# Reordering the last loads and the middle weight load of a two-layer decode attention kernel, with the program order of the last head pair to match

## The chip, the cores and the metric

The kernel runs on one core of one Trainium2 chip. The metric is the device time of one execution in microseconds (us). A profile is one further execution, and its clock starts at the span's start. Its page is the summary that the profiler prints of it. Engines: PE is the tensor engine, PEld its weight load, DVE the vector engine, ACT the scalar engine, SP the engine that issues the loads.

The runs were spread over several chips. Ratios are always taken against the kernel before, on the same chip and in the same rounds. The profiles shown are single executions.

## The reference

Two independent decode attention layers, A and B, of the same shape, each for one token (cut; A and B differ only in their data):

```python
# x [1,1,512], k_cache and v_cache [1,32,8192,128], wq [512,4096], wo [4096,512], all bf16
q = (x @ wq).reshape(B, Sq, H, Dh).transpose(0, 2, 1, 3)
scores = einsum("bhqd,bhkd->bhqk", q, k_cache) * Dh ** -0.5
p = softmax(scores, axis=-1)
o = einsum("bhqk,bhkd->bhqd", p, v_cache)
out = o.transpose(0, 2, 1, 3).reshape(B, Sq, H * Dh) @ wo
# result: concatenate([out_A, out_B], axis=-1)
```

K and V of both layers are 64 heads of 2 MB each; with the weights 285 MB are read once. There is hardly any arithmetic per byte.

## The kernel before

The heads are taken in 32 pairs (16 of A, then 16 of B). K of pair j is called Kj, V of pair j is Vj; each is a 4 MB load. All loads go through one ring of five 4 MB slots in a fixed order, and a load is issued as soon as the load five places earlier has been used up:

```python
order = [('wq', a) for a in range(NA)]
for j in range(NPR + 1):                   # NPR = 32 pairs, PPA = 16 pairs a layer
    if j < NPR:
        order.append(('k', j))
    if 1 <= j <= NPR:
        if j == NPR:
            order.append(('wo', NA - 1))   # woB, between V30 and V31
        order.append(('v', j - 1))
    if j == PPA:
        order.append(('wo', 0))            # woA, behind V15
LAST_PARTS = [(0, 64), (64, 96), (96, 112), (112, 128)]   # V31 comes in four loads
...
if n >= NS:                                # NS = 5 slots
    for ctr, val in free_of[n - NS]:
        W('SP', ctr, val)
```

For a pair, DVE multiplies K by q in eight pieces (`plan_M`), PE sums over parts of the head dimension with an identity matrix (`plan_fold`, two halves of 16 matmuls), DVE reduces (`plan_R`), and a softmax follows over DVE, PE and ACT (`plan_m1` to `plan_ri`). `plan_PV` multiplies V by p: 128 matmuls of two columns, each with its own 128x128 weight load. `plan_o` scales. `plan_w` permutes the result of a block of heads on PE and DVE, and `plan_y` multiplies it with rows of wo.

Every engine runs its own list in the order in which the plan functions were called. The order of before (cut):

```python
for j in range(NPR + 1):
    ...                                    # M(j), fold(j,0) .. softmax of j-1 .. fold(j,1), R(j,0)
    if j == NPR:                           # behind the last pair's softmax:
        for h0, n, pm in wo_plan[NA - 1]:  # w and y of B's heads 0..27 (16 + 8 + 4)
            if pm and (NA - 1) * PPA + (h0 + n) // 2 - 1 <= j - 2:
                plan_w(NA - 1, h0, n)
                plan_y(NA - 1, h0, n, pm)
    if c:
        plan_PV(j - 1)
    if j == PPA + 1:                       # j = 17: w and y of A behind PV of pair 16
        for h0, n, pm in wo_plan[0]:
            plan_w(0, h0, n)
            plan_y(0, h0, n, pm)
plan_o(NPR - 1)
for h0, n, pm in wo_plan[NA - 1]:          # y of B's last four heads
    if not pm:
        plan_y(NA - 1, h0, n, pm)
```

## Time and profile before

Median 691.01 us (690.29 to 692.37, three runs). The span of the profile is 688.0 us.

| what | number | read from |
|---|---|---|
| HBM bytes | 285.2 MB, 415 GB/s over the span | the page, part 3 |
| rate where the stream is full | 423 to 437 GB/s in nearly all slices | the page, row GB/s |
| DVE idle for K loads | most of 179.4 us, 6 us a pair | the page, groups |
| nothing issued by SP | 360.1 to 395.0 us | timeline of SP |
| last landing, y_sb, end | 675.8, 683.2, 688.0 us | completions, timeline |

The page's row of GB/s in 40 slices of 17.2 us, and two of its groups (line, engine, operation, tiles, count, then busy us and mean ns, then idle time before them and its releaser):

```profile
GB/s 366 440 433 436 423 426 430 430 437 430 431 428 430 428 430 430 432 429 435 432 428 426 371 425 396 420 430 428 431 428 433 424 433 433 430 432 431 421 408 47
L360 DVE TENSOR_TENSOR ring<-ring,qbc 128x2048 bf16<-128x2048 bf16 x256 | 300.7, 1215 | 179.4 <-DMA ring<-in_B_k_cache_dram 93.1
L458 PE MATMUL otps<-p,ring 128*128 128x2 bf16 x4096 | 108.2, 163 | 0.6 <-issue 0.6
```

The stream is flat but for the first slice, a dip in the middle (371, 396) and the last slices. The Trainium skill, "DMA: Bandwidth & Descriptors", section Specifications, gives a fabric ceiling of 435 GB/s; the trace agrees, with about 430 in most slices.

The dip, in the timeline of SP's issues (start, duration, what), and in windows of 5 us (window, length, busy of PE, PEld, DVE, ACT, POOL with counts, granted PE clock with 1.00 for full speed, DMA share, GB/s):

```profile
356.92 0.33 SPq L262 DMA_DIRECT2D ring<-in_B_k_cache_dram  x1
360.11 0.33 SPq L262 DMA_DIRECT2D ring<-in_B_v_cache_dram  x1
394.97 0.33 SPq L262 DMA_DIRECT2D ring<-in_B_k_cache_dram  x1
```

```profile
385.00:390.00 5.00, 2.93 (x110) 2.72 (x106) 2.36 (x4) 0.00 (x0) 0.00 (x0) 0.90 1.02 436
390.00:395.00 5.00, 4.40 (x128) 4.35 (x128) 0.41 (x2) 0.00 (x0) 0.00 (x0) 0.50 0.61 259
395.00:400.00 5.00, 0.26 (x1) 0.13 (x2) 5.00 (x7) 0.00 (x0) 0.00 (x0) 0.50 0.86 321
```

SP has nothing to issue for 35 us, because K19 needs the slot of woA and woA is used up only by y of A, which PE ends at 395. The queue runs dry on the way.

The tail, in the chain of work that ended last (start, duration, what):

```profile
609.17 35.89 DMA ring<-in_B_k_cache_dram
...
658.83 5.21 PE fold L373 x16
664.03 3.21 PE otps L458 x128
...
667.42 0.61 DVE s_sb L386
...
671.21 0.58 PE stps L435 x2
671.80 0.43 PE qwps L496 x16
672.23 1.02 issue
673.25 2.26 PE yps L536 x64
...
678.80 3.43 PE otps L458 x128
...
682.47 0.71 PE yps L536 x16
683.21 0.16 DVE y_sb L545
```

K31 lands at 645.06. The last fold ends at 664, then come PV of pair 30, the softmax of pair 31 (to 671.8), w and y of 28 heads (to 678.8) and all of PV of pair 31, though V31 had landed at 675.8.

### The profile page before, as it was taken

What the parts mean: (1) busy time and instruction counts of PE and PEld (TensorE: products, weight loads), DVE (VectorE), ACT (ScalarE), POOL (GpSimd) and SP (SyncE); (2) the same over time, 40 slices, a digit from 0 to 9 for tenths busy, and PEclk for the clock granted to TensorE, in tenths of its full rate; (3) what the DMA queues carried; (4) which work ended last, traced back from release to release, by engine and by line L of the source; (5) the groups of instructions that cost most, each with busy time, mean ns of one, the idle gap of its engine ahead of it and who ended that gap; (6) DMA issues with size and microseconds to landing.
All of it is one profiled execution on the core that took longest, in us unless ns stands there. A gap on an engine that the chain in (4) does not pass through costs nothing.

```text
span 688.0 us, 12357 instructions
## 1 busy us (share of the span) xinstructions
PE 467.0 (68%) x5660; PEld 260.8 (38%) x5660; DVE 377.6 (55%) x513; ACT 42.5 (6%) x169; POOL 2.4 (0%) x16
## 2 busy tenths in 40 slices
PE   0487687767776766766683767756776676777675
PEld 0134443433444433433341634423443442443345
DVE  4158655664655566646535385566565456664621
ACT  0110000000000000000000000000000000000010
POOL 1000000000000000000000000000000000000000
PEclk9999877987778776888776878777788776788775
DMA  9999999999999999999999899999999999999991
GB/s 366 440 433 436 423 426 430 430 437 430 431 428 430 428 430 430 432 429 435 432 428 426 371 425 396 420 430 428 431 428 433 424 433 433 430 432 431 421 408 47
DMA packets 11667, 286.00 MB, mean 416 GB/s; under 512 B 1760, under 2 KB 2272, under 8 KB 2656
## 3 DMA queue, kind: packets, MB, share of 16 engines
q1 hardware_dynamic: 11328, 285.22, 97.1%
q8 instruction: 44, 0.72, 0.4%
q10 hardware_dynamic: 288, 0.00, 0.0%
q14 instruction: 7, 0.06, 0.0%
HBM read 285.21 MB, written 0.00 MB: 415 GB/s over the span
## 4 chain that ended last, share of the span: by engine, by line
DMA 57%; PE 28%; DVE 11%; issue 2%; ACT 1%; ACTq 0%; DVEq 0%
DMA ring<-in_B_k_cache_dram 27%; DMA ring<-in_A_k_cache_dram 26%; PE fold L373 17%; DVE ring L360 10%; PE otps L458 6%; DMA xT<-in_B_x_dram 3%; PE qwps L332 2%; PE yps L536 1%; ACT qbc L339 1%; DVE m L409 1%; ACT p L428 0%; DVE wt L503 0%; DVE w_bf L512 0%; PE stps L404 0%; PE qwps L496 0%
## 5 line engine op out<-in xcount | busy, mean ns | idle before, releaser
L360 DVE TENSOR_TENSOR ring<-ring,qbc 128x2048 bf16<-128x2048 bf16 x256 | 300.7, 1215 | 179.4 <-DMA ring<-in_B_k_cache_dram 93.1
L373 PE MATMUL fold<-ring,ident 128*128 128x512 bf16 x1024 | 308.3, 469 | 126.5 <-DVE ring L360 126.4
L373 PEld LDWEIGHTS fold<-ring,ident 128*128 128x128 bf16 x1024 | 114.0, 117 | 295.6 <-DVE ring L360 131.9
L458 PEld LDWEIGHTS otps<-p,ring 128*128 128x128 bf16 x4096 | 108.3, 96 | 8.0 <-issue 0.7
L458 PE MATMUL otps<-p,ring 128*128 128x2 bf16 x4096 | 108.2, 163 | 0.6 <-issue 0.6
L386 DVE TENSOR_REDUCE s_sb<-fold 128x64 f32<-128x512 f32 x64 | 42.9, 671 | 7.5 <-PE fold L373 7.2
L409 DVE TENSOR_REDUCE m<-stps 2x1 f32<-2x128 f32 x32 | 8.9, 279 | 67.4 <-PE stps L404 67.4
L420 ACT COPY nb<-stps 128x1 f32<-128x1 f32 x32 | 5.1, 159 | 586.2 <-PE stps L414 586.2
L435 PE MATMUL stps<-rowsum,ones_f 128*128 128x2 f32 x64 | 12.6, 267 | 41.5 <-ACT p L428 41.5
L332 PE MATMUL qwps<-ring,xsel 128*128 128x512 bf16 x64 | 16.5, 405 | 29.3 <-DVE xsel L225 24.4
L428 ACT ACTIVATE p<-s_sb,nb 64x128 bf16<-64x128 f32 x64 | 27.9, 436 | 2.1 <-ACT nb L420 0.3
L435 PEld LDWEIGHTS stps<-rowsum,ones_f 128*128 128x128 f32 x64 | 9.9, 194 | 44.2 <-ACT p L428 44.2
L332 PEld LDWEIGHTS qwps<-ring,xsel 128*128 128x128 bf16 x64 | 6.0, 103 | 39.3 <-issue 27.3
L414 PE MATMUL stps<-m,sel 2*128 2x1 f32 x64 | 12.3, 259 | 11.9 <-DVE m L409 11.9
L414 PEld LDWEIGHTS stps<-m,sel 2*128 2x128 f32 x64 | 9.6, 186 | 24.5 <-DVE m L409 24.5
L396 DVE TENSOR_REDUCE m<-s_sb 64x1 f32<-64x128 f32 x64 | 17.7, 277 | 1.0
L474 DVE TENSOR_TENSOR ot<-otps,rinv 128x2 bf16<-128x2 f32 x32 | 4.9, 152 | 15.6 <-PE otps L458 15.6
L428 ACT ACTIVATION_READ_ACCUMULATOR p<-s_sb,nb 64x1 f32 x64 | 11.7, 182 | 0.0
L536 PE MATMUL yps<-w_bf,ring 128*128 128x1 bf16 x240 | 8.6, 172 | 3.8 <-DVE w_bf L512 2.8
L536 PEld LDWEIGHTS yps<-w_bf,ring 128*128 128x128 bf16 x240 | 8.3, 118 | 4.1 <-issue 2.9
L404 PE MATMUL stps<-ident_f,m 128*2 128x128 f32 x32 | 8.7, 273 | 1.5 <-DVE m L396 1.5
L225 DVE TENSOR_SCALAR xsel<-parity,xT 128x256 bf16<-128x256 bf16 x8 | 1.7, 282 | 12.2 <-DMA xT<-in_B_x_dram 12.2
(30 smaller groups left out, 34.9 us busy)
## 6 DMA issues: line engine op xcount, KB each, us to landing
ring<-in_A_k_cache_dram SPq DMA_DIRECT2D x16, 4096.0 KB, 37.2
ring<-in_A_v_cache_dram SPq DMA_DIRECT2D x16, 4096.0 KB, 31.9
ring<-in_B_k_cache_dram SPq DMA_DIRECT2D x16, 4096.0 KB, 37.7
ring<-in_B_v_cache_dram SPq DMA_DIRECT2D x15, 4096.0 KB, 32.4
ring<-in_A_wq_dram SPq DMA_DIRECT2D x1, 4096.0 KB, 12.5
ring<-in_B_wq_dram SPq DMA_DIRECT2D x1, 4096.0 KB, 22.0
ring<-in_A_wo_dram SPq DMA_DIRECT2D x1, 4096.0 KB, 38.8
ring<-in_B_wo_dram SPq DMA_DIRECT2D x1, 2048.0 KB, 33.3
```

Of the source, the lines that this page charges most:

```text
L332: m = e.matmul(qw_ps[:, :].rearrange("p (j d) -> p j d", d=Dh), xsel[:, a, c, par, :], wq[:, c, 4 * g:4 * g + 4, par, :], start=(i == 0), ...
L360: m_val[(j, i)] = INC('DVE', c_m, lambda e: e.tensor_tensor(t, t, qbc[:, a, jj:jj + 1, :].broadcast_to([P, CH, Dh]), ALU.mult))
L373: m = e.matmul(fold_ps[h][:, :].rearrange("p (t e) -> p t e", e=FE), ident[:], t[:, h * HT:(h + 1) * HT, c * FE:(c + 1) * FE], start=(c == ...
L386: r_val[(j, h)] = INC('DVE', c_r, lambda e: e.tensor_reduce(s_sb[:, j % 2, h * HT:(h + 1) * HT], fold_ps[h][:, :].rearrange("p (t e) -> p ...
L396: m1_val[j] = INC('DVE', c_m1, lambda e, h=h, q0=q0, q1=q1: e.tensor_reduce(m1[q0:q1, j % 2, h:h + 1], s_sb[q0:q1, j % 2, :], AX.X, ALU.max))
L404: tr_val[j] = INC('PE', c_tr, lambda e: e.transpose(st_ps[j % 2][0:2, 0:P], m1[:, j % 2, :], ident_f[:]))
L409: m2_val[j] = INC('DVE', c_m2, lambda e: e.tensor_reduce(m2[0:2, j % 2:j % 2 + 1], st_ps[j % 2][0:2, 0:P], AX.X, ALU.max))
L414: bc_val[j] = INC('PE', c_bc, lambda e: e.matmul(st_ps[j % 2][:, P:P + 1], sel2[:], m2[0:2, j % 2:j % 2 + 1], start=True, stop=True))
L428: e_val[j] = INC('ACT', c_e, lambda e, h=h, q0=q0, q1=q1: e.activation(p2[q0:q1, j % 2, :, h], s_sb[q0:q1, j % 2, :], AF.Exp, bias=nb[q0:q ...
L435: s_val[j] = INC('PE', c_s, lambda e: e.matmul(st_ps[j % 2][:, P + 2:P + 4], ones_f[:], rowsum[:, j % 2, :], start=True, stop=True))
L458: m = e.matmul(ot_ps[j % 2][:, 0:2], t[:, i, :], p2[:, j % 2, i, :], start=(i == 0), stop=(i == TP - 1))
L536: m = e.matmul(y_ps[:, b:b + 1], wo[:, h0 + i, :, b], src[:, a, h0 + i:h0 + i + 1], start=(first and i == 0 and b == 0), stop=(lastblk and ...
```

## The change

Its intent has two parts. In the middle, woA is loaded two pairs later (behind V17) and y of A is done one pair later, so that no load waits for y of A while the queue runs dry. At the end, the loads come in the order K31, woB, V30, V31, and everything that needs neither V30 nor V31 (the softmax of pair 31, y of 28 heads) is planned ahead of PV of pair 30. The core of the diff:

```diff
-            if 1 <= j <= NPR:
-                if j == NPR:
-                    order.append(('wo', NA - 1))
+            if j == NPR - 1:
+                order.append(('wo', NA - 1))
+            if j >= 1:
                 order.append(('v', j - 1))
-            if j == PPA:
+            if j == PPA + 2:
                 order.append(('wo', 0))
 ...
+                if j == PPA + 1:
+                    for h0, n, pm in wo_plan[0]:
+                        plan_w(0, h0, n)
+                if j == PPA + 2:
+                    for h0, n, pm in wo_plan[0]:
+                        plan_y(0, h0, n, pm)
 ...
+        j = NPR - 1
+        plan_R(j, 1)
+        plan_w_ready(j - 2)
+        ys = list(perm_l)
+        plan_y(LA, *ys.pop(0))
+        plan_m1(j)
+        plan_tr(j)
+        if ys:
+            plan_y(LA, *ys.pop(0))
+        plan_m2(j)
+        plan_bc(j)
+        plan_exp(j)
+        plan_sum(j)
+        plan_ri(j)
+        for b in ys:
+            plan_y(LA, *b)
+        for i in range(2):
+            plan_PV(j - 1 + i)
+            plan_o(j - 1 + i)
+            plan_y(LA, *direct_l[i])
```

(B's last four heads become two blocks of two; w of B's heads is done in the loop as soon as its o is there.)

More of the change, by code (lines that the diff above doesn't have):

```diff
@@ L92, in bass_concat_heads__mha_block_cached__gqa_block_cached__decode_kernel @@
             h0 += n
-        if h0 < H:
-            blocks.append((h0, H - h0, False))
+        while h0 < H:
+            blocks.append((h0, 2, False))
+            h0 += 2
         wo_plan.append(blocks)
@@ L560, in bass_concat_heads__mha_block_cached__gqa_block_cached__decode_kernel, with plan_w_ready @@
                 plan_q(a, g)
-        for j in range(NPR + 1):
-            k = j < NPR
+        LA = NA - 1
+        perm_l = [b for b in wo_plan[LA] if b[2]]
+        direct_l = [b for b in wo_plan[LA] if not b[2]]
+        w_done = set()
+        def plan_w_ready(jo):
+            for h0, n, pm in perm_l:
+                if h0 not in w_done and LA * PPA + (h0 + n) // 2 - 1 <= jo:
+                    w_done.add(h0)
+                    plan_w(LA, h0, n)
+        for j in range(NPR):
             c = 0 <= j - 1
-            if k:
-                for i in range(4):
-                    plan_M(j, i)
+            for i in range(4):
+                plan_M(j, i)
             if j >= 2:
@@ L570, in bass_concat_heads__mha_block_cached__gqa_block_cached__decode_kernel @@
                 plan_R(j - 1, 1)
-            if k:
-                plan_fold(j, 0)
-                plan_M(j, 4)
+            plan_fold(j, 0)
+            plan_M(j, 4)
             if c:
@@ L576, in bass_concat_heads__mha_block_cached__gqa_block_cached__decode_kernel @@
                 plan_tr(j - 1)
-            if k:
-                plan_M(j, 5)
+            plan_M(j, 5)
             if c:
@@ L583, in bass_concat_heads__mha_block_cached__gqa_block_cached__decode_kernel @@
                 plan_sum(j - 1)
-            if k:
-                plan_M(j, 6)
-                plan_M(j, 7)
+            plan_M(j, 6)
+            plan_M(j, 7)
             if c:
                 plan_ri(j - 1)
-            if k:
-                plan_fold(j, 1)
-                plan_R(j, 0)
-            if j == NPR:
-                for h0, n, pm in wo_plan[NA - 1]:
-                    if pm and (NA - 1) * PPA + (h0 + n) // 2 - 1 <= j - 2:
-                        plan_w(NA - 1, h0, n)
-                        plan_y(NA - 1, h0, n, pm)
-            if c:
-                plan_PV(j - 1)
-            if j == PPA + 1:
-                for h0, n, pm in wo_plan[0]:
-                    plan_w(0, h0, n)
-                    plan_y(0, h0, n, pm)
-        plan_o(NPR - 1)
-        for h0, n, pm in wo_plan[NA - 1]:
-            if not pm:
-                plan_y(NA - 1, h0, n, pm)
+            plan_fold(j, 1)
+            plan_R(j, 0)
+            if j < NPR - 1:
+                if c:
+                    plan_PV(j - 1)
+                if j == PPA + 1:
[7 more added lines that the diff above has]
+        plan_R(j, 1)
+        plan_w_ready(j - 2)
+        assert len(w_done) == len(perm_l)
+        ys = list(perm_l)
[11 more added lines that the diff above has]
+            plan_y(LA, *b)
+        assert len(direct_l) == 2
+        for i in range(2):
+            plan_PV(j - 1 + i)
+            plan_o(j - 1 + i)
+            plan_y(LA, *direct_l[i])
         assert issued[0] == len(queue)
```

## The prediction

> **What bounds it now.** Loads. The page's GB/s row is flat at 423 to 437 in nearly all slices (Trainium skill, "DMA: Bandwidth & Descriptors", Specifications: fabric ceiling 435 GB/s; the trace agrees). 285.2 MB at 430 GB/s is 663 of the 688 us span. The groups show DVE idle 179 us for K loads, about 6 us per head pair. Three things lie outside the stream:
>
> 1. Start, about 13 us. Not touched.
> 2. A drain in the middle. The timeline of SP shows no load issued from 360.1 to 395.0 us: K19 needs woA's slot, which only y of A releases. The chain: PV ends at 386.9, w on DVE to 390.4, y matmuls 4.4 us to 395.0. The windows from 390 to 396 us show 262, 279, 205 GB/s, then 328 and 377: 1.4 MB short, about 3.2 us.
> 3. The tail. K31 lands at 645.06, V31's parts at 671.0, 673.3, 674.6, 675.8. PE does, in order: fold to 663.7, PV30 to 667.2, softmax of pair 31 (to 671.8), w and y of 28 heads (to 678.8), all of PV31 (3.4 us), o, y of 4 heads; y_sb at 683.2, end 688.0. Half of the 12 us after the last byte is work that needs neither V30 nor V31.
>
> **What the change does.** Same bytes, one more DMA (B's last 4 heads in two blocks).
>
> - Middle: woA goes behind V17, its y one pair later. K19 now hangs on K17; the load that hangs on woA (K21) is released while K19, V18, K20 and V19 are queued. w of A holds DVE 3 to 5 us before K18's products; the queue is deep enough there. Gain: the drain, about 3.0 us. A dip at 428 to 432 us (262 GB/s, DMA busy; the 1 KB store of A lands about there) moves but stays.
> - End: landings become K31, woB, V30, V31. K31 lands at about 642, V31's last part 30.7 us after it. From K31's landing = 0, with durations of before: fold ends 18.6; w of 4 and y of 16 heads (2.3) to 21.2 while DVE does R and max; transpose, y of 8 heads (1.2), bc, exp, sum to 25.2; y of 4 heads to 25.9; PV30 3.4 to 29.4 (V30 landed at about 20); o, y of 2 heads to 30.1; PV31 3.4 to 33.5 (its last part landed at 30.7: PE ends it, not the load); o, y, y_sb at 34.4, against 38.15 before. The store, 4.6 to 4.8 us, stays. Gain: about 3.7 us.
>
> All of it is on the path: 6.7 to 7 us, 1.0%.
>
> **Predicted:** 684.0 us, 8 times in 10 between 681.5 and 687.0. Faster by over 2% (below 677.2) 0.04, within 2% 0.94, slower 0.02.
>
> **What would show it.** SP's issues without the 35 us gap, windows at 380 to 410 us near 430 GB/s, no 34 us wait of SP for y. K31 landing near 642. In the timeline of the tail: y of 16 heads right after the last fold, PV31 within 1 us of PV30's end, y_sb 34 us after K31's landing, the last data landing about 3 us before y_sb instead of 8.
>
> **What would make it wrong.** SP's queue seems limited in descriptors (one V31 issue took 15.1 us with woB's many 1 KB packets queued); with woB ahead of V30, V30's issue may be held. I expect no gap in the stream; one would cost directly. [...] If the drain comes back at K21, only 3.7 us remain (687). Reaching 2% would need 7 us more from the stream, where nothing changes.

## The result

The changed kernel takes 682.62 us (682.46 to 683.23), the kernel before 690.79. The ratio is 0.988, interval 0.9862 to 0.9897; a second measurement on another chip (run after_again below) gives 0.9897. The saving is 1.0 to 1.2%, 7 to 8 us.

The profile after, same views. The span is 680.7 us.

```profile
GB/s 370 431 430 431 431 433 429 429 430 430 427 435 433 428 430 432 430 426 430 431 430 429 431 430 430 428 405 432 429 432 432 428 426 430 430 430 433 422 415 131
```

```profile
360.37 0.33 SPq L263 DMA_DIRECT2D ring<-in_A_wo_dram  x1
377.37 0.33 SPq L263 DMA_DIRECT2D ring<-in_B_k_cache_dram  x1
380.56 0.33 SPq L263 DMA_DIRECT2D ring<-in_B_v_cache_dram  x1
400.58 0.33 SPq L263 DMA_DIRECT2D ring<-in_B_k_cache_dram  x1
```

```profile
385.00:390.00 5.00, 1.43 (x4) 0.59 (x5) 5.00 (x7) 0.00 (x0) 0.00 (x0) 0.50 1.02 439
390.00:395.00 5.00, 4.63 (x17) 1.78 (x14) 2.69 (x6) 0.00 (x0) 0.00 (x0) 0.74 0.99 426
395.00:400.00 5.00, 3.49 (x18) 1.73 (x18) 2.53 (x4) 1.14 (x5) 0.00 (x0) 1.00 1.02 439
```

The gap of SP and the drain are gone. A dip of 405 GB/s is left in the 27th slice, where the 1 KB store of A lands.

```profile
656.47 3.63 PE fold L374 x16
660.10 0.08 PE qwps L497 x4
660.18 2.14 PE yps L537 x64
...
665.35 0.58 PE stps L436 x2
665.93 0.52 PE yps L537 x16
666.46 3.43 PE otps L459 x128
...
670.13 0.43 PE yps L537 x8
670.56 0.32 PE otps L459 x12
670.88 1.51 issue
672.39 3.25 PE otps L459 x116
...
676.35 0.16 DVE y_sb L546
```

y of 16 heads stands behind the last fold, PV of the two last pairs come together, and the copy to y_sb starts 1.5 us after the last landing (674.88) instead of 7.4 us. There is one gap that nobody planned, 1.5 us of "issue" in the middle of PV of pair 31.

One thing did not fit. The drain was gone, yet K31, which I had expected near 642, landed at 643.7, only 1.4 us earlier than in the profile before, while the tail from K31 to y_sb shrank from 38.15 to 32.65 us, by 5.5 us. The predicted terms were 3.0 and 3.7. The sum was right; in this pair of profiles the parts were not.

The completions tell more. The Trainium skill, "DMA: Bandwidth & Descriptors", section "Why a DMA increments its semaphore by 16 and not by 1", says that a load is split over up to 16 DMA engines which finish independently, and that only the full 16 means that all data landed. The trace has these 16 increments. For K31, sorted (us; computed from the trace's semaphore events, which do not say which DMA engine each is):

```
before  641.3 641.3 641.4 641.6 641.6 641.7 642.2 642.2 644.5 644.6 644.7 644.7 644.8 644.8 645.0 645.1
after   634.9 635.0 635.2 635.3 635.5 635.6 636.2 638.8 642.2 643.2 643.3 643.3 643.5 643.6 643.6 643.7
```

DVE starts when the sixteenth is in. The fastest DMA engines gained 6.3 us from the change, the slowest 1.4 us. The spread at V31's last part (last completion minus first) is 4.8 us before and 10.1 us after.

What spreads them can be read in the same trace. The first row below has the times at which blocks of 16 KB of instructions start to be fetched in one stretch (44 in all; the profile's queue q8). The others have, for the loads of that stretch, the first of the 16 completions and the sum over all 16 of their lag behind it:

```
after: fetches at 321.7, 340.7, 357.9, 376.1, 382.6
first completion 323.6  333.3  343.0  352.7  362.4  372.1  381.8  391.5
sum of lags       36.1   36.1   37.7   37.7   40.2   40.5   43.8   44.2
```

The sum stands still, within 0.4 us, where no block is fetched and steps up by about 1.6 us for each one. (The step of 2.5 us at 362.4 has a second part: the trace has a smaller block of instructions, 8 KB on q14, at 362.7.) Over the profile a line through all loads but the first few gives 1.8 us a block, with a correlation of 0.999; the few q14 blocks and A's store are in that slope. The single lags show what a fetch does. The loads with their first completions at 518.4 and 528.1 us differ by one block, fetched at 528.7 while the second was landing: of the sixteen lags one goes from 7.1 to 8.6 us, and the others stay within 0.1 us. So a fetch sets one DMA engine back by about 1.5 us, and it stays back. The late ones are about half of the sixteen: at V31's last part seven lags are under 2 us, one is 4.6, eight are 7.1 to 10.1. The Trainium skill, "Runtime: NRT & Kernel Launch", section Instruction fetch mechanics, says that instructions are refilled in 16 KiB blocks of 256, which agrees: PE's 11320 matmuls and weight loads are 44.2 such blocks. It says also that the cost of crossing into a new block is "mostly hidden". This trace shows a cost elsewhere that is not: the load that has to share its DMA engine with a block is late, and PE and DVE wait for the latest of 16.

### The profile page after: what moved, and what is told of

Same layout as the page of the kernel before. It is cut to its first block, busy times and chain, and to the rows that moved or that the text cites. A ratio compares the mean times of both kernels' runs of the same rounds, so it can differ in the third digit from the quotient of the medians.

```text
span 680.7 us, 12357 instructions
## 1 busy us (share of the span) xinstructions
PE 479.8 (70%) x5660; PEld 264.9 (39%) x5660; DVE 377.8 (56%) x513; ACT 42.5 (6%) x169; POOL 2.4 (0%) x16
## 4 chain that ended last, share of the span: by engine, by line
DMA 53%; PE 30%; DVE 12%; issue 3%; ACT 1%; ACTq 0%; DVEq 0%
DMA ring<-in_B_k_cache_dram 27%; DMA ring<-in_A_k_cache_dram 22%; PE fold L374 19%; DVE ring L361 11%; PE otps L459 7%; DMA xT<-in_B_x_dram 3%; PE qwps L333 2%; PE yps L537 1%; ACT qbc L340 1%; DVE m L410 1%; ACT p L429 0%; PE stps L436 0%; PE stps L405 0%; DVE wt L504 0%; PE stps L415 0%
## 5 line engine op out<-in xcount | busy, mean ns | idle before, releaser
L374 PE MATMUL fold<-ring,ident 128*128 128x512 bf16 x1024 | 320.5, 484 | 109.7 <-DVE ring L361 109.2
L374 PEld LDWEIGHTS fold<-ring,ident 128*128 128x128 bf16 x1024 | 117.3, 120 | 287.8 <-issue 117.5
L436 PEld LDWEIGHTS stps<-rowsum,ones_f 128*128 128x128 f32 x64 | 10.8, 211 | 44.2 <-ACT p L429 44.2
L504 DVE TENSOR_TENSOR wt<-qwps,hmask 128x512 f32<-128x512 f32 (+3 forms) x5 | 2.2, 440 | 24.6 <-PE qwps L497 24.5
```

Of the source, the lines that this page charges most:

```text
L374: m = e.matmul(fold_ps[h][:, :].rearrange("p (t e) -> p t e", e=FE), ident[:], t[:, h * HT:(h + 1) * HT, c * FE:(c + 1) * FE], start=(c == ...
L436: s_val[j] = INC('PE', c_s, lambda e: e.matmul(st_ps[j % 2][:, P + 2:P + 4], ones_f[:], rowsum[:, j % 2, :], start=True, stop=True))
```

## The experiments

Two theories stood against each other for the middle. P, the prediction's: the drain cost the time that the stream lacked, 3.0 us. S: only the faster DMA engines had run dry, so the slowest one gained little, and the gain at the end was larger than predicted. For the spread, S says instruction fetches; its rival R says that some DMA engines are slower by themselves. All kernels were correct unless it is said otherwise.

### The two halves, and the whole again

mid_only takes the kernel before and changes only the middle:

```diff
-            if j == PPA:
+            if j == PPA + 2:
                 order.append(('wo', 0))
             if j == PPA + 1:
                 for h0, n, pm in wo_plan[0]:
                     plan_w(0, h0, n)
-                    plan_y(0, h0, n, pm)
+            if j == PPA + 2:
+                for h0, n, pm in wo_plan[0]:
+                    plan_y(0, h0, n, pm)
```

> Only the middle part of the change (woA behind V17, y of A one pair later), the end as before. Theory P (as predicted): the drain cost 3.0 us of stream, so the time falls by about 3 us (688 us) and K31 lands at 642. Theory S (the drain gave the slowest of the 16 DMA engines little to lose, because only the faster ones ran dry): the first of the 16 completions of K31 comes about 6 us earlier (641.3 to about 635), the last only 1.0 to 1.5 us earlier (645.06 to about 643.7), the spread of the 16 at V31's last part grows from 4.8 to about 10 us, and the time falls by only about 1.3 us (689.5 us).

end_only is the changed kernel with the middle part undone (woA behind V15, y of A at j = 17).

> Only the end part of the change, the middle as before. Theory P: gain 3.7 us (687 us). Theory S: the end is worth 5 to 6 us (about 685.5 us), K31 lands at 645.1 as before, the spread at V31's last part stays near 5 us, and y_sb comes 32 to 33.5 us after K31's landing.

> The changed kernel once more, beside its two halves on the same chip: 682.5 us, ratio 0.988; sum of the two halves' gains within 1 us of its gain, under both theories.

before_again is the kernel before, for a second profile of it (one run, on another chip).

> The kernel before, profiled once more, to see how far one profile's landings can be trusted. Expected: the drain again between about 390 and 400 us, fastest completion of the next load at 406 to 409, spread under 1 us just after it and about 5 us at V31's last part, K31's last completion between 645 and 648.

Times, on one chip for the first three: mid_only 687.33 us, ratio 0.9949 (0.9928 to 0.9971); end_only 687.14, 0.9947 (0.9927 to 0.9966); after_again 683.84, 0.9897 (0.9876 to 0.9918). Times the mean of before (about 690.5), that is 3.5, 3.7 and 7.1 us. The halves add up, and each has the size that P gave it. The landings, us:

| profile | drain | K31 first / last completion | V31's last part, last (spread) | y_sb | K31's landing to y_sb |
|---|---|---|---|---|---|
| before | yes | 641.3 / 645.1 | 675.8 (4.8) | 683.2 | 38.1 |
| before_again | yes | 644.3 / 648.4 | 678.7 (4.7) | 684.5 | 36.1 |
| end_only | yes | 644.0 / 648.0 | 679.2 (5.6) | 681.9 | 33.9 |
| mid_only | no | 634.6 / 643.5 | 674.1 (9.7) | 681.5 | 38.0 |
| after | no | 634.9 / 643.7 | 674.9 (10.1) | 676.4 | 32.7 |
| after_again | no | 635.4 / 644.8 | 675.7 (10.4) | 679.4 | 34.5 |

Neither theory is right as it stood. S's signature is all there: the fast engines gain 8 us on average (643.2 to 635.0), the spread doubles to about 10 us, the slowest gains much less. But the slowest gains 3.1 us on average (three profiles with the drain 647.1, three without 644.0; mid_loads, mid_program and tail_tune below, which share the new middle, have 643.7, 644.6 and 644.1), because the drain differs from run to run. In all three profiles with it, the spread falls across it from over 5 us to 0.7 us or less: the slow engines catch up. In the windows of before_again it is deeper than in the first profile:

```profile
385.00:390.00 5.00, 4.87 (x150) 4.15 (x148) 0.03 (x1) 0.00 (x0) 0.00 (x0) 1.00 1.04 446
390.00:395.00 5.00, 2.54 (x75) 2.47 (x76) 2.73 (x4) 0.00 (x0) 0.00 (x0) 0.60 0.60 252
395.00:400.00 5.00, 2.45 (x74) 2.36 (x71) 2.52 (x4) 0.00 (x0) 0.00 (x0) 0.50 0.41 121
```

There SP's first issue after the gap came at 397.5 us instead of 395.0. Counted as bytes missing at 430 GB/s from 385 to 410 us, which is how the prediction priced it, the drain is 3.0 us in before, 5.6 in before_again and 5.3 in end_only. At the load right after it, the slowest engine is 0.6, 3.0 and 3.0 us later than in the mean of the three profiles without it (406.6). So the missing bytes overstate what the slowest engine loses; the prediction's 3.0 came from the shallowest of the three drains. Of the mean of 3.1 us at K31, the load right after the drain has 2.2; about 1 us more comes at the two or three loads around A's store, whose dip costs less without the drain. The tail shrinks from 37.4 us on average (38.1, 36.1, 38.0) to 33.7 (33.9, 32.7, 34.5), by 3.7. So the first pair of profiles, with 1.4 and 5.5, was a lucky before against a lucky after; the mean of three shows the predicted sizes, though for the middle not by the predicted step. The profile after had its last fold at 3.63 us; after_again took 5.15 us for it, like before (5.21), and ended its tail 34.5 us after K31, as predicted:

```profile
658.47 5.15 PE fold L374 x16
...
669.71 3.43 PE otps L459 x128
...
675.41 3.25 PE otps L459 x116
...
679.36 0.16 DVE y_sb L546
```

### The end: loads alone, program alone

mid_loads has the middle part and, of the end, only the new order of loads; mid_program has the middle part and only the new program:

```diff
 # mid_loads against mid_only
-                if j == NPR:
-                    order.append(('wo', NA - 1))
+            if j == NPR - 1:                 # ahead of V30 instead of V31
+                order.append(('wo', NA - 1))
 # mid_program against the changed kernel
-            if j == NPR - 1:
+            if j == NPR:
                 order.append(('wo', NA - 1))
```

> The middle part, and of the end part only the order of the loads (K31, woB, V30, V31), with the program of before. PE then waits with PV30 for V30 (about 21 us after K31), and softmax of pair 31 and the 7 us of w and y stand behind it: PV30 ends at 24.5, softmax at 29, y at 36, PV31 at 39.6, y_sb at about 40.5 after K31's landing. So slower than the middle part alone by about 2.5 us: 690 us, ratio to before about 1.0.

> The middle part, and of the end part only the program (softmax of pair 31 and y of 28 heads ahead of PV30), with the loads in the old order (V30, woB, V31). y of 16 heads then waits for woB, about 21 us after K31, instead of starting at 18, and softmax stands behind it: some 1.5 to 2.5 us slower than the whole change where PE is what ends it: 685 to 686 us.

mid_loads took 690.85 us, ratio 1.0009 (0.9985 to 1.0033): the loads alone give back all of the middle's gain. mid_program took 685.4 us, ratio 0.9930 (0.9903 to 0.9957). In their profiles the waits that each theory named are there (mid_loads first, then mid_program):

```profile
664.67 3.45 PE L458 MATMUL otps<-p,ring 128*128 128x2 bf16 x128 [2.68 <-DMA ring<-in_B_v_cache_dram]
```

```profile
664.60 2.29 PE L537 MATMUL yps<-w_bf,ring 128*128 128x1 bf16 x64 [0.76 <-DMA ring<-in_B_wo_dram]
```

With the loads alone, PE stands before V30 with the softmax and 7 us of y behind it. With the program alone, it stands before woB. By the ratios, the program alone takes 0.2% off the middle part's 0.9949 (the intervals overlap), the loads alone add 0.6%, and both together take off 0.5 to 0.7%: the new order of loads costs time without the new program, and most of the gain comes with the pair.

### Instruction fetches and the spread

half_pv is the changed kernel without every second PV matmul; its result is wrong (relative error 0.57). The loads are the same.

```diff
                 for i in range(t0, t1):
+                    if i % 2 and i != TP - 1:
+                        continue
                     m = e.matmul(ot_ps[j % 2][:, 0:2], t[:, i, :], p2[:, j % 2, i, :],
```

> The changed kernel with every second PV matmul left out (a wrong result on purpose): same loads, 4000 PE instructions fewer (2016 matmuls with their weight loads), so about 16 of the 44 blocks of instructions fewer to fetch. Theory S with fetches as its cause: the spread of V31's last part falls from 10.1 us to about 6 or 7, its last landing comes 3 us earlier (672), the time falls by 3 to 4 us. Rival R (the slow DMA engines are slow by themselves): the spread stays at 10 us, the last landing at about 675, and the time falls only by the shorter PV31, at most 1 us.

wide_pv does PV of pairs 0 to 29 with 32 matmuls that stream four tiles of V each, and gives a correct result; mixed_pv does so in 13 pairs only:

```diff
+                for g in range(TP // 4):
+                    m = e.matmul(
+                        ot_ps[j % 2][0:8, :].rearrange("p (t d) -> p t d", d=Dh),
+                        p2[:, j % 2, 4 * g:4 * g + 4, :].rearrange("p t h -> p (t h)"),
+                        t[:, 4 * g:4 * g + 4, :], start=(g == 0), stop=(g == TP // 4 - 1))
 ...                                        # ACT copies [8,512] to pvs; PE takes the diagonal:
+                for t in range(4):
+                    m = e.matmul(st_ps[j % 2][:, P + 4:P + 6],
+                                 pvs[:, j % 2, t * Dh:(t + 1) * Dh],
+                                 ident_f[0:8, 2 * t:2 * t + 2], start=(t == 0), stop=(t == 3))
 # mixed_pv:
+        WIDE = {j for j in range(0, NPR - 2, 2) if j not in (16, 18)}
```

> The changed kernel with PV of pairs 0 to 29 as 32 matmuls that move 512 columns (four tiles of V against eight columns of p; four small matmuls pick the diagonal), correct result. About 5300 PE instructions fewer, so about 20 fewer blocks of 16 KB to fetch. If fetches of instructions hold back single DMA engines by about 1.5 us each (theory S): the spread at V31's last part falls from 10.4 to about 5 or 6 us, its last landing to 670 to 671, the time to 679 to 681. If they do not (R): spread 10, time 683 to 684. If PE becomes the bound (PV takes 6.8 us or more a pair instead of 3.4), slower than 690.

> The changed kernel with the wide PV (32 matmuls) in 13 pairs only (every second one, none near y of A), so that PE stays under the 19.4 us a pair that the loads take. 2288 PE instructions fewer, about 9 blocks: theory S expects 35 instead of 44 blocks, a spread at V31's last part of 7 to 8.5 us instead of 10.4, its last landing about 1.5 to 2.5 us earlier (672.5 to 673.5), and a time of 681 to 683 us, less where PE's own chain ends the kernel. R expects a spread of 10 and no gain.

| run | blocks fetched | spread at V31's last part | its last completion | time | ratio to before |
|---|---|---|---|---|---|
| after / after_again | 44 | 10.1 / 10.4 | 674.9 / 675.7 | 682.6 / 683.8 | 0.988 / 0.9897 |
| mixed_pv | 35 | 8.2 | 673.0 | 681.6 | 0.9871 (0.9849 to 0.9894) |
| half_pv | 29 | 6.5 | 671.0 | 678.4 | 0.9822 (0.9802 to 0.9842) |

The blocks, as the pages of after and half_pv count them (queue, kind: packets, MB, share of 16 engines):

```profile
q8 instruction: 44, 0.72, 0.4%
```

```profile
q8 instruction: 29, 0.48, 0.3%
```

The spread is 0.22 to 0.24 us a block in all of them. half_pv makes PE's work shorter and mixed_pv makes it longer, so what they share is the fetches. R falls. The last landing of half_pv is 4.6 us ahead of that of after_again on the same chip, and its y_sb 7.2 us (672.2 against 679.4); by median its time is 5.4 us shorter. The other 2.5 us of y_sb are the shorter PV of the tail: with it, V31's loads and no longer PE end the kernel, and PE waits for each part:

```profile
669.84 0.38 PE L461 MATMUL otps<-p,ring 128*128 128x2 bf16 x8 [0.65 <-DMA ring<-in_B_v_cache_dram]
671.08 0.40 PE L461 MATMUL otps<-p,ring 128*128 128x2 bf16 x9 [0.87 <-DMA ring<-in_B_v_cache_dram]
672.20 0.16 DVE L548 CAST y_sb<-yps 128x4 bf16<-128x4 f32 x1 [0.52 <-PE yps L539]
```

It also has no gap inside PV of pair 31. That the 1.5 us of "issue" there (1.3 us in after_again) is PE waiting for its own next block is likely, since in the profile after one started to be fetched at 669.9 us, just ahead of it, and in after_again, end_only and one_store the gap opens before the same matmul, 1.0 to 1.2 us after a fetch began; but no run took it apart.

wide_pv as a correct version for all pairs failed: 719.72 us, ratio 1.0414. Its page:

```profile
PE 582.5 (82%) x3020; PEld 262.3 (37%) x3020; DVE 377.2 (53%) x513; ACT 59.7 (8%) x199; POOL 2.5 (0%) x16
L464 PE MATMUL otps<-ring,p 128*8 128x512 bf16 x960 | 212.1, 379 | 0.0
```

960 of these matmuls take 212 us, 7.1 us a pair against 3.4, and the chain of PE and DVE then takes longer than the loads. The spread falls to 0.45 us, but that tells nothing, as its loads no longer run back to back.

### Two smaller trials on what ends the kernel now

tail_tune fills PE's two waits for exp with y:

```diff
                 plan_exp(j - 1)
+                if j == NPR - 1:
+                    plan_y(LA, *perm_l[0])    # 16 heads, ahead of the last fold
                 plan_sum(j - 1)
 ...
         plan_exp(j)
-        plan_sum(j)
-        plan_ri(j)
         for b in ys:
             plan_y(LA, *b)                    # 4 heads
+        plan_sum(j)
+        plan_ri(j)
```

> The changed kernel with y of the first 16 heads moved into PE's wait for exp of pair 30 (ahead of the last fold) and y of 4 heads into its wait for exp of pair 31. PE's work between the last fold and PV30 falls from 6.1 us to about 3.3 us (w, transpose, y of 8, bc, y of 4, sum). Where PE ends the kernel (the second profile of the changed kernel: y_sb 3.7 us after the last landing) y_sb moves forward by 2 to 2.8 us, until PV30 waits for V30 or the last matmuls for V31's last part; where the loads end it (the first profile) by at most 0.3 us. Time: 681 to 682.5 us, 1 to 2 us under the changed kernel.

683.85 us, ratio 0.9885 (0.9862 to 0.9909): no gain that the interval shows, and not the 681 to 682.5 us that was expected. The chain of its profile shows one reason:

```profile
655.83 2.23 PE yps L537 x64
658.05 0.42 PE stps L436 x2
658.48 6.40 PE fold L374 x16
```

The last fold took 6.40 us instead of 5.15 (after_again) or 3.63 (after), and the granted clock in 658.5 to 664.9 us was 0.55, against 0.70 during the last fold of after_again. PE was busy with 64 matmuls of one column right before it. The Trainium skill, "TensorE: Matmul & The Clock Gate", Part 1, says that a monitor of activity sets the clock and that about 3.4 us of sustained work release it. In after_again the trace agrees: the clock fell at 658.2 us, the fold began at 658.5, and the clock was back at 661.6. In tail_tune it fell at 657.4, before y had ended, and was back only at 664.3, though the fold ran from 658.3 on. One profile: that narrow matmuls count for little is argued, not shown, and that the steps of the clock fell badly by chance is not excluded, since in the profile after the clock stayed full through the whole fold (3.63 us). The matmuls of y themselves took 172 ns each at half clock and at full clock.

one_store leaves out A's own store and sends both halves at the end, and mixed_store does that on top of mixed_pv:

```diff
+                if a < NA - 1:
+                    return
                 W('SP', c_ye, ve)
 ...
-                            out[0, 0, a * NOUT:(a + 1) * NOUT].rearrange("(p b) -> p b", b=NB),
-                            y_sb[:, a, :])
+                            out[0, 0].rearrange("(a p b) -> p a b", a=NA, b=NB), y_sb[:])
```

> The changed kernel without A's own 1 KB store: both halves leave in one store at the end. The dip of the stream near 440 us (0.9 to 1.5 us, counted over all DMA engines) should be gone and V31's last part land 0.5 to 1 us earlier (674 to 674.5). Where PE ends the kernel, less comes of it; the last store has twice the packets and may take some tenths longer. Time 682.5 to 683.5, at most 1 us under the changed kernel.

> The wide PV in 13 pairs and the single store together: 35 blocks and no dip. Last landing about 672.3, time 680.5 to 681.5, ratio to before about 0.986; if both effects are real, a little under the wide PV alone.

one_store took 684.0 us, ratio 0.9899 (0.9878 to 0.9920), just over the expected range. The dip is gone and the last landing is at 673.7, but PE ends the kernel (y_sb 677.8, 4.1 us later), so the time is that of the changed kernel. mixed_store took 681.78 us, ratio 0.9865 (0.9842 to 0.9889), again just over, with the last landing at 672.1 and y_sb at 676.2. It and mixed_pv have the lowest ratios of the correct kernels, but their intervals overlap with those of the changed kernel; a version that clearly beats it was not found.

## Why the prediction was right

- **Time.** 684.0 us was predicted, 682.6 (and 683.8 on another chip) was measured, inside the range of 681.5 to 687.0. Within 2% was given 0.94 and came.
- **What bounds it.** Right: SP's gap is gone, the windows at 385 to 400 us read 426 to 439 GB/s, and SP's wait for y fell from 34.5 to 5.9 us in the view of its waits.
- **Middle, 3.0 us.** The size holds (3.5 us by time, 3.1 us in K31's landing over three profiles on each side), but the step behind it was wrong, and that the size holds is partly luck. The prediction took the bytes missing in the stream for the time lost. In fact the 16 DMA engines lose different amounts: the drain let the slow ones catch up with the fast ones, and without it the spread grows to 10 us. By the prediction's own count a mean drain would have been worth 4.6 us (3.0, 5.6, 5.3); it started from the shallowest, and left out about 1 us that the dip of A's store gives. The fast ones gained 8 us on average (643.2 to 635.0 in K31's first completion), the slow ones 3. "K31 landing near 642" was off for this reason (643.7).
- **Tail, 3.7 us.** The size holds as a mean (37.4 to 33.7 us). In single profiles it moves by 1 to 2 us, with the clock that PE was granted in the last folds (the last one took 5.21 us in before, 3.63 in before_again). The prediction took the length of those folds from one profile.
- **The dip of A's store.** "Moves but stays" was right. It also shrank: counted over all DMA engines from about 1.7 us to 0.9 us in the first two profiles. one_store shows that what is left of it is worth nothing while PE ends the kernel.
- **What ends it.** "PE ends it, not the load" held in after_again (y_sb 3.7 us after the last landing) and only just in the profile after (1.5 us). The 1.5 us gap inside PV of pair 31 was not foreseen; the faster folds of that profile hid it.
- **SP's queue of descriptors.** Feared, no gap came of it (the issues of V30 and V31 took up to 3.5 us, against 15.1 us for one before): but for the dip of A's store, the slices stay at 415 GB/s or more to the last but one.

## What to carry to other kernels

A load is only as early as the slowest of its 16 DMA engines, so bytes missing from a stream's average rate are not the time lost (5.3 to 5.6 us missing in two profiles here, 3.0 us lost by the slowest); compare the first and the last completion of a load before you price a drain. In this kernel's stream, which never pauses, every fetched block of instructions set one DMA engine back by about 1.5 us for good, so on a kernel bound by loads the number of instructions can delay the last load, even if they are those of an engine with slack: 15 blocks fewer brought it 3.8 to 4.6 us earlier. How much of that becomes time depends on what ends the kernel; mixed_pv's 9 blocks gained no time that the intervals show. Split a gain into terms only with several profiles on each side: one pair can give the right sum from wrong parts.

## What the Trainium skill lacked or had wrong

- "Runtime: NRT & Kernel Launch", Instruction fetch mechanics, calls the cost of crossing a block "mostly hidden" and says nothing of the loads that share a DMA engine with it. Here each of the 44 blocks adds 1.5 to 1.8 us to the summed lag of a load's 16 completions, and a kernel with 15 blocks fewer and the same loads has its last landing 3.8 to 4.6 us earlier.
- No page says that a stream without pauses lets the DMA engines drift apart: 10 us at the end of 680 us, against 5 us with one drain in the middle.
- "DMA: Bandwidth & Descriptors", Queues, rings and completion order, puts the refill on row 14. In these traces the 44 blocks of 16 KB are on q8, and q14 has 7 to 9 smaller packets of instructions; that the trace's queue numbers are the page's rows is assumed.
- "TensorE: Matmul & The Clock Gate" gives about 3.4 us of sustained work for the release of the clock and does not say whether one-column matmuls count. In tail_tune the clock fell to half near the end of 2.3 us of them and stayed there for 6.8 us, 5.9 of them under a fold; no run settles why.
- No page prices a 1 KB store of 8-byte packets inside a full load stream: 0.5 to 2.5 us of the stream in these traces (bytes missing at 430 GB/s from 425 to 465 us), 0.1 us when it is moved to the end.
